# A margin on the PSUM banks in a hand-planned order of attention scores and a gated MLP

## The chip, the cores and the metric

The kernel runs on one core of a Trainium2 chip. The metric is device time in microseconds (us) for one execution, the median of several; lower is better. Three runs of the kernel before gave 2689.28, 2691.16 and 2694.49 us.

## The reference

One transformer-like block over 2048 rows of 576 columns, all in float32. The normalised rows go through an attention with 32 heads of 18 columns and, beside it, through a bilinear gated MLP with 4608 hidden columns; the two results are multiplied.

```python
def _A_ref(x, wqkv, wo):
    qkv = (x @ wqkv).reshape(B, S, 3, H, Dh) ...
    scores = jnp.einsum("bhqd,bhkd->bhqk", q, k) * (Dh ** -0.5)
    p = _softmax(scores, axis=-1)
    o = jnp.einsum("bhqk,bhkd->bhqd", p, v)
    return o.transpose(...).reshape(B, S, D) @ wo
def _B_ref(x, w_gate, w_up, w_down):
    g = jnp.einsum("bsd,df->bsf", x, w_gate)
    u = jnp.einsum("bsd,df->bsf", x, w_up)
    return jnp.einsum("bsf,fd->bsd", g * u, w_down)
xn = _layernorm(x)
return x + _A_ref(xn, A_wqkv, A_wo) * _silu(_B_ref(xn, B_w_gate, B_w_up, B_w_down))
```

## The kernel before

A first stage normalises the rows, projects q, k and v and writes them to DRAM. A last stage multiplies by `wo` and joins the two branches. Between them lies the main stage, from about 208 to 2610 us of the profiled execution, and everything that the change touches is in it.

Every float32 operand is carried as a high and a low part, so a product is a sum of three. In the main stage the 128 rows of the TensorE array are used as two halves of 64 rows, row group 0 and row group 64, which work at the same time on different matmuls. TensorE's instructions stand in one queue, and each matmul is preceded there by the load of its weights (LDWEIGHTS). The work of the stage is this:

- **First-pass scores** (`a_item`, L558): per head 64 matmuls of 54 rows by 512 columns into a PSUM bank `pa`, of which there are two, used in turn. VectorE reduces each bank to its row maxima (L560). A head's maxima are written back into the operand of the second pass (`max_rows`).
- **Second-pass scores** (`b_item`, L591): again 64 per head, into `pb`, also two banks in turn; ScalarE takes the exponential out of the bank (L593).
- **Up and gate products** (`gu_op`, L654): tiles of 27 matmuls of 512 columns into one of four banks `pg`; ScalarE (L659) or VectorE (L666) empties it. Row group 0 makes the up tiles, row group 64 the gate tiles.
- **Down products** (`down_op`, L682): tiles of 12 matmuls of 288 columns into a bank `pg`, which VectorE adds to the sums (L710; L708 for the first of a block).
- **Visits** (`visit`, `pv_group`, L602): the product of the exponentials with v, for four tiles of keys as a rule. These use the array in four column strips and not in two row groups, so both row groups stop for them. VectorE (L608) or ScalarE (L606) empties their `pg` bank.

A long matmul is one of 512 columns in a row group, a short one has 288 (`LONG, SHORT = 0.2335, 0.1335` at L783, in us).

**The order is planned when the program is built.** `order()` (L1010) keeps a clock for each row group (`clk`), the times at which VectorE, ScalarE and GpSimd will be free (`free`, `engine()`), and for each bank the time at which it may be used again (`banks`, `next_free()`). At each step it takes the row group whose clock is behind and emits one instruction for it: the next matmul of its stream (`stream()`: up or gate tiles and down tiles), or a score. The first-pass scores go to row group 0 and the second-pass scores to row group 64, with few exceptions. A score is emitted when its bank is free by the plan and its goal has come; the goals lie `pace` apart, so that the scores of all heads are spread over the stage (`a_goal`, `b_goal`). If neither can go, the clock is moved on. Nothing of the plan's times is in the program: what it leaves behind is the sequence on each engine, and on the chip each instruction waits for the semaphores of what it really needs. An instruction that waits holds what stands behind it in its queue.

Before the change a bank is usable 0.03 us after the plan's end of the operation that empties it, in four places (L883, L908, L960, L1056), and a score may be emitted up to 0.02 us ahead of that (L1042):

```python
banks["a"][slot] = engine("DVE", issue(r, LONG), 0.60) + 0.03      # L883
at, goal, score, can = next_free("a"), a_goal(na) + lean, a_next, na < TOTAL and na < nb + N + MOST   # L1032
blocked = op is not None and op[1] and next_free("g") > clk[r]     # L1041
```

The pace is worked out from a sum of the matmuls' lengths, `part`, and a term for the 512 (head, tile) pieces of the visits (L859 to L862).

Of the kernel before, what the change touches and what calls it, by code (L numbers as in the profile page):

```python
# [40 lines left out]
def kernel(  # L41
# [13 lines left out]
    H = 32  # L55
# [484 lines left out]
    with ExitStack() as mid:  # L540
# [283 lines left out]
        N = 64  # L824
        TOTAL = H * N
        LEAD, MOST = 24, 40
        PACE, SKEW, PULL, FIRST, ROWS = 1.01, 3.0, 3.0, 2.0, 6.0
        slots, gone = [0, 0], [0.0, 0.0]
        clk, free = [0.0, 0.0], {"DVE": 0.0, "ACT": 0.0, "POOL": 0.0}
# [10 lines left out]
        def engine(eng, start, taken):  # L840
            free[eng] = max(free[eng], start) + taken
            return free[eng] + TAIL[eng]

        def issue(r, length):

            at = issued[0] = max(clk[r], issued[0])
            clk[r] = at + length + (0.11 if fresh[r] else 0.0)
            fresh[r] = False
            return at + (0.456 if length == LONG else 0.356)
# [7 lines left out]
        there, queue = {}, [0.0]  # L857
        na = nb = 0
        part = len(units) * (2 * 27 * LONG + 4 * 12 * SHORT) + (TOTAL + N + LEAD) * LONG  # L859
        span = part + H * NT * (0.859 - 0.01)  # L860
        QUICK, LAST = 0.75, 0.75
        pace = (PACE * span - QUICK * N - LAST * (N + LEAD)) / (TOTAL - N)  # L862

# [8 lines left out]
        def a_next(r=0):  # L872
            nonlocal na
            h, i = divmod(na, N)
            if i == 0 and 2 <= h + 1 < H:
                stacks.append((0, h + 1))
            if i == 48 and (0, h + 1) in stacks:
                stacks.remove((0, h + 1))
                load_stack(0, h + 1)
            a_item(h, i, r)  # L880
            slot = turn["a"] % 2
            turn["a"] += 1
            banks["a"][slot] = engine("DVE", issue(r, LONG), 0.60) + 0.03  # L883
            na += 1
            if i == N - 1:
                max_fold(h)
                max_rows(h)
                rows_done[h] = engine("DVE", 0.0, 0.85) + ROWS
# [5 lines left out]
        def b_next(r=1):  # L894
            nonlocal nb
            h, i = divmod(nb, N)
            if i == 0 and h < H - 1:
                stacks.append((64, h + 1))
            if i == 48 and (64, h + 1) in stacks:
                stacks.remove((64, h + 1))  # L900
                load_stack(64, h + 1)
            if i == 16 and h % 2 == 0 and h // 2 + 1 < H // 2:
                load_v(h // 2 + 1)
            b_item(h, i, r)
            slot = turn["b"] % 2
            turn["b"] += 1
            end = engine("ACT", issue(r, LONG), 0.495)
            banks["b"][slot] = end + 0.03  # L908
            nb += 1
            if i % 4 == 3:  # L910
                due.append((h, i // 4, end + 0.03))
# [24 lines left out]
        def visit(now):  # L936

            now = max([now, *clk] + [j[0] for j in jobs])
            done = list(jobs)
            many = 0  # L940
            now += 0.095
            if due:
                now = max(now, next_free("g"))
            for j in done:
                jobs.remove(j)
                j[1](j[2])
                now += 0.6
                engine("DVE", now + 0.2, 0.8)
            for h, t, at in due:
                if at > now + 0.5 * many + 0.3 or h != due[0][0]:  # L950
                    break
                now += 0.859
                many += 1
            if many:
                k = banks["g"].index(next_free("g"))
                h = due[0][0]
                ts = [t for _, t, _ in due[:many]]
                pv_group(h, ts, k)
                end = engine("DVE", now + 0.25, 0.60) if ts[0] else engine("ACT", now + 0.25, 0.495)
                banks["g"][k] = end + 0.03  # L960
                if ts[-1] == NT - 1:
                    if h // 4 < H // 4 - 1:
                        finish(h)
                        engine("DVE", end, 1.45)
                    else:
                        jobs.append((end + 0.2, finish, h))
                del due[:many]
            clk[0] = clk[1] = issued[0] = now + 0.13
            fresh[:] = True, True
# [40 lines left out]
        def order():  # L1010
            nonlocal na, nb
            load_v(0)
            feeds = [stream(0), stream(1)]
            heads.extend(next(f) for f in feeds)
            wait = None
            while any(heads) or na < TOTAL or nb < TOTAL or due or jobs:
                now = max(clk)
                small(now)
                need = 4 if nb < TOTAL or any(heads) and not stuck[0] else 1
                if (len(due) >= need and due[need - 1][2] <= now  # L1020
                        or any(j[0] + (3.0 if due else 1.0) <= now for j in jobs)
                        or jobs and not any(heads) and na == TOTAL):
                    wait = now if wait is None else wait
                    if abs(clk[0] - clk[1]) < 0.04 or now > wait + 1.0 or not all(heads):
                        visit(now if any(heads) else max([now] + [j[0] for j in jobs] + [d[2] for d in due]))
                        wait = None
                        continue
                r = 0 if clk[0] <= clk[1] else 1
                lean = PULL * (gone[0] - gone[1] - SKEW) * (1 if r else -1)

                if r == 0 and (na < TOTAL or nb < TOTAL - N) or r == 1 and nb == 0 and na < N:
                    at, goal, score, can = next_free("a"), a_goal(na) + lean, a_next, na < TOTAL and na < nb + N + MOST  # L1032
                    can = can and not late(goal, r)
                else:
                    at, goal, score, can = next_free("b"), b_goal(nb) + lean, b_next, b_ready(r)
                op = heads[r]
                held = op is not None and not can_go(r, op[1], op[4])
                stuck[0] = held and heads[1 - r] is not None and not can_go(1 - r, heads[1 - r][1], heads[1 - r][4])
                if held:
                    op = None  # L1040
                blocked = op is not None and op[1] and next_free("g") > clk[r]  # L1041
                if can and (at <= clk[r] + 0.02 and (goal <= clk[r] or blocked) or op is None and (at <= clk[r] or not held)):  # L1042
                    clk[r] = max(clk[r], at)
                    score(r)
                elif op is not None:
                    length, first, work, end, (kind, n, k) = op
                    if first:
                        clk[r] = max(clk[r], next_free("g"))
                        slots[r] = banks["g"].index(next_free("g"))
                        banks["g"][slots[r]] = 1e9  # L1050
                    work()
                    lands = issue(r, length)
                    gone[r] += length
                    if end:
                        done = engine(end[0], lands, end[1])
                        banks["g"][slots[r]] = done + 0.03  # L1056
                        if kind == "d":
                            if k == 47:
                                parts.setdefault(n, []).append(clk[r])
                                if len(parts[n]) == 2:  # L1060
                                    downed[n] = moved(max(parts[n]) + 0.3, 1.18) if (n + 1) % NF2 else 0.0
                        elif r == 0:
                            upped[n] = done
                        else:
                            gated[n] = done
                            fin = engine("ACT", done + 0.05, 0.535)
                            fin = engine("POOL", fin + 0.05, 1.29)
                            loaded[n] = moved(done - 0.4, 1.18) if (n // 2 + 1) % NF2 else 0.0
                            lands = moved(fin, 0.524)
                            if n % 2:  # L1070
                                there["h", n // 2] = lands
                            if stacks:
                                load_stack(*stacks.pop(0))
                                moved(fin + 1.4, 0.88)
                    heads[r] = next(feeds[r], None)
                else:
                    clk[r] = max(clk[r] + 0.05, min(clk[1 - r] + 0.01, clk[r] + 0.3))
# [113 lines left out]
```

## Time and profile before

| | |
|---|---|
| runs of the kernel before | 2689.28, 2691.16, 2694.49 us |
| the profiled execution | 2687.2 us, of which 2685.4 us are its span |
| granted TensorE clock, mean | 0.997 |
| ScalarE L593, exponentials | 2048 of 597 ns, 1167.1 us busy |
| VectorE L560, maxima | 2048 of 685 ns, 1356.8 us busy |
| VectorE L710, down tiles | 544 of 445 ns, 233.4 us busy |

A row such as "L560 ... x2048 | 1356.8, 685" gives the line, the engine, what it writes and reads, how many there were, the busy time in us and the mean length of one in ns. PE is a matmul and PEld a weight load; the profiler models a matmul's end, so its start is the better number. In a timeline a row is a start, a length, an engine and a line, and rows of one kind that follow each other are merged ("x9"). In brackets stands how long the engine sat idle before, and what ended it. In the view of the waits a row gives who waited for whom, the sum in us, how often, and the longest; idle time under 0.15 us isn't listed there.

### The profile page before, as it was taken

The numbers are of one execution on the slowest core, as the hardware profiler recorded it, in microseconds if no ns is written. First come the engines' busy times: TensorE is split into PE (matmuls) and PEld (weight loads), VectorE is DVE, ScalarE is ACT, GpSimd is POOL, SyncE is SP. The second block draws the span as 40 slices with busy tenths as digits, with TensorE's granted clock in tenths as the row PEclk, the third lists the DMA queues.
The fourth block names the chain that finished last, engine by engine and source line by source line (L and its number), as shares of the span: only waits on it lengthen the run. The fifth ranks groups of instructions, "written<-read, shape, count | busy, mean of one in ns | idle before, by whom it ended". The sixth has DMA issues, their size and how long they took to land.

```text
span 2685.4 us, 59017 instructions
## 1 busy us (share of the span) xinstructions
PE 2649.1 (99%) x24456; PEld 2053.7 (76%) x24456; DVE 1917.8 (71%) x3384; ACT 1476.2 (55%) x2726; POOL 451.2 (17%) x414
## 2 busy tenths in 40 slices
PE   7999999999999999999999999999999999999998
PEld 5898777777777777777777777777777777777778
DVE  7217777777777787777777787777777787777536
ACT  3222666666665565565555555555555565555552
POOL 2113333333311111111001101000001111000005
PEclk9999999999999999999999999999999999999999
DMA  6799978888785656676676656566586565654555
GB/s 209 222 296 268 255 216 222 220 221 223 206 225 153 178 161 172 188 201 181 161 180 165 172 150 181 164 172 169 158 199 165 169 174 156 180 159 152 154 178 200
DMA packets 212820, 508.62 MB, mean 189 GB/s; under 512 B 71112, under 2 KB 130888, under 8 KB 179016
## 3 DMA queue, kind: packets, MB, share of 16 engines
q1 hardware_dynamic: 209512, 493.64, 65.9%
q0 software_dynamic: 3040, 11.21, 1.1%
q8 instruction: 192, 3.15, 0.5%
q14 instruction: 76, 0.62, 0.1%
HBM read 314.05 MB, written 109.97 MB: 158 GB/s over the span
## 4 chain that ended last, share of the span: by engine, by line
PE 93%; DVE 3%; DMA 2%; issue 1%; ACT 1%; POOL 1%; SPq 0%; POOLq 0%; ACTq 0%; DVEq 0%
PE pg L654 32%; PE pg L602 17%; PE pg L682 15%; PE pa L558 12%; PE pb L591 8%; PE pg L1148 2%; PE pg L373 2%; PE pa L319 2%; PE pb L319 2%; DMA xc<-sx 1%; DVE mx L560 1%; DVE xn L282 0%; DMA draw<-in_B_w_down_dram 0%; POOL wgu L192 0%; DVE st L271 0%
## 5 line engine op out<-in xcount | busy, mean ns | idle before, releaser
L593 ACT ACTIVATE pt<-pb 128x512 f32<-128x512 f32 x2048 | 1167.1, 597 | 686.6 <-PE pb L591 541.5
L560 DVE TENSOR_REDUCE mx<-pa 128x1 f32<-128x512 f32 x2048 | 1356.8, 685 | 247.4 <-PE pb L591 114.0
L654 PE MATMUL pg<-xc,wgu 64*128 64x512 f32 x7776 | 1387.8, 394 | 4.4 <-DMA xc<-sx 3.8
L654 PEld LDWEIGHTS pg<-xc,wgu 64*128 64x128 f32 x7776 | 993.3, 186 | 88.4 <-DMA xc<-sx 7.0
L558 PE MATMUL pa<-ks,qs 54*128 54x512 f32 x2048 | 830.4, 414 | 0.1
L591 PE MATMUL pb<-qs,ks 56*128 56x512 f32 x2048 | 820.0, 412 | 1.8 <-ACT pt L593 1.8
L682 PE MATMUL pg<-wd,hs 64*128 64x288 f32 x6816 | 775.3, 294 | 3.3 <-DVE acc L710 3.3
L682 PEld LDWEIGHTS pg<-wd,hs 64*128 64x128 f32 x6816 | 731.8, 185 | 28.6 <-issue 13.4
L558 PEld LDWEIGHTS pa<-ks,qs 54*128 54x128 f32 x2048 | 370.7, 184 | 168.0 <-issue 83.8
L670 POOL TENSOR_TENSOR hs<-us,hs 128x512 fp32r<-128x512 f32 x144 | 185.8, 1291 | 1804.9 <-ACT hs L669 1754.5
L602 PE MATMUL pg<-pt,vt 128*32 128x512 f32 x4096 | 466.4, 595 | 0.6 <-DVE acc L708 0.2
L591 PEld LDWEIGHTS pb<-qs,ks 56*128 56x128 f32 x2048 | 366.5, 184 | 27.4 <-ACT pt L593 10.8
L602 PEld LDWEIGHTS pg<-pt,vt 128*32 128x32 f32 x4096 | 119.8, 109 | 266.4 <-issue 260.0
L608 DVE TENSOR_TENSOR oc<-oc,pg 128x512 f32<-128x512 f32 x98 | 67.4, 688 | 310.0 <-PE pg L602 310.0
L710 DVE TENSOR_TENSOR acc<-acc,pg 128x288 f32<-128x288 f32 x544 | 233.4, 445 | 27.1 <-PE pg L682 25.0
L669 ACT ACTIVATE hs<-us 128x512 fp32r<-128x512 f32 x144 | 91.0, 632 | 159.0 <-DVE us L666 154.2
L192 POOL TENSOR_TENSOR wgu<-wraw,wgu 128x384 fp32r<-128x384 f32 x108 | 108.0, 1015 | 104.8 <-ACT wgu L191 76.5
L666 DVE TENSOR_TENSOR us<-pg,us 128x512 f32<-128x512 f32 x144 | 98.2, 682 | 23.2 <-PE pg L654 22.8
L659 ACT ACTIVATE us<-pg 128x512 f32<-128x512 f32 x144 | 86.1, 598 | 39.8 <-PE pg L654 27.7
L606 ACT ACTIVATE oc<-pg 128x512 f32<-128x512 f32 x32 | 19.1, 598 | 103.3 <-PE pg L602 103.3
L223 POOL TENSOR_TENSOR wd<-draw,wd 128x576 fp32r<-128x576 f32 x36 | 51.1, 1431 | 90.9 <-ACT wd L222 88.7
L323 DVE TENSOR_TENSOR hl<-pb,hl 128x512 fp32r<-128x512 f32 x18 | 12.4, 690 | 72.2 <-ACT hl L322 72.2
(104 smaller groups left out, 1071.3 us busy)
## 6 DMA issues: line engine op xcount, KB each, us to landing
wgu<-swg SPq DMA_DIRECT2D x102, 1152.0 KB
hs<-hs SPq DMA_DIRECT2D x288, 256.0 KB
wd<-swd SPq DMA_DIRECT2D x50, 1152.0 KB
swg<-wgu SPq DMA_DIRECT2D x36, 1152.0 KB
qs<-sqk SPq DMA_DIRECT2D x192, 144.0 KB
ks<-sqk SPq DMA_DIRECT2D x192, 144.0 KB
swd<-wd SPq DMA_DIRECT2D x18, 1152.0 KB
sqk<-hl SPq DMA_DIRECT2D x32, 512.0 KB
```

The source lines that it names most:

```text
L192: nc.gpsimd.tensor_tensor(w[:, 9 + b:12 + b, :], raw[:, b:b + 3, :], w[:, b:b + 3, :].bitcast(FT), op=OP.subtract)
L319: nc.tensor.matmul(p, wq[b, a], xcs[c][:, e, :], start=n == 0, stop=n == len(PAIRS) - 1)
L558: nc.tensor.matmul(p, q[rows, t * 128:(t + 1) * 128], k[rows, c * 512:(c + 1) * 512], start=True, stop=True)
L560: nc.vector.tensor_reduce(mx[h][:, t, c:c + 1], p, axis=AX.X, op=OP.max)
L591: nc.tensor.matmul(p, k[rows, t * 128:(t + 1) * 128], q[rows, c * 512:(c + 1) * 512], start=True, stop=True)
L593: nc.scalar.activation(pt[t, c // 2][:, c % 2, :], p, AF.Exp, scale=scale)
L602: nc.tensor.matmul(p[32 * c:32 * c + 32, :], vt[h // 2][:, t, 6 * (h % 2):6 * (h % 2) + 32], pt[t, c // 2][:, c % 2, :], start=t == ts[0], ...
L654: nc.tensor.matmul(ps, gw[n][half[r], a, :], xg[i][half[r], e, :], start=k == 0, stop=k == len(TERMS) - 1)
L666: nc.vector.tensor_tensor(h32, ps, h32, op=OP.mult)
L670: nc.gpsimd.tensor_tensor(hj[:, 1, :], h32, hj[:, 0, :].bitcast(FT), op=OP.subtract)
L682: nc.tensor.matmul(ps[:, 0:HALF], hs[u][half[r], k, j, a, s * 128:(s + 1) * 128], dw[u][half[r], k, j, e, :], start=n == 0, stop=n == len( ...
L710: nc.vector.tensor_tensor(a, a, ps[:, 0:HALF], op=OP.add)
```

## The change

A constant `EARLY = 0.17` takes the place of 0.03 at the four places where a bank's next use is noted. The tolerance for a score falls from 0.02 to 0.01 us. `visit` takes the margin off again where it sets its own time. In the pace, the length of a visit's piece is taken as 0.859 - 0.04 and not 0.859 - 0.01 us, so that `span` is 512 x 0.03 = 15.4 us shorter and two scores' goals lie about 0.008 us closer together (1.01 x 15.4 / 1984). No instruction is added or removed in number: the same matmuls, evictions and transfers are emitted, in another order.

```diff
+        EARLY = 0.17
...
-        span = part + H * NT * (0.859 - 0.01)
+        span = part + H * NT * (0.859 - 0.04)
...
-            banks["a"][slot] = engine("DVE", issue(r, LONG), 0.60) + 0.03
+            banks["a"][slot] = engine("DVE", issue(r, LONG), 0.60) + EARLY
...
-            banks["b"][slot] = end + 0.03
+            banks["b"][slot] = end + EARLY
...
             if due:
-                now = max(now, next_free("g"))
+                now = max(now, next_free("g") - EARLY + 0.03)
...
-                banks["g"][k] = end + 0.03
+                banks["g"][k] = end + EARLY
...
-                if can and (at <= clk[r] + 0.02 and (goal <= clk[r] or blocked) or op is None and (at <= clk[r] or not held)):
+                if can and (at <= clk[r] + 0.01 and (goal <= clk[r] or blocked) or op is None and (at <= clk[r] or not held)):
...
-                        banks["g"][slots[r]] = done + 0.03
+                        banks["g"][slots[r]] = done + EARLY
```

## The prediction

> **What bounds the kernel now.** I read the page first, then the groups by line, the waits, the chain and timelines of some microseconds.
>
> ```profile
> span 2685.4 us, 59017 instructions
> ...
> PE 2649.1 (99%) x24456; PEld 2053.7 (76%) x24456; DVE 1917.8 (71%) x3384; ACT 1476.2 (55%) x2726; POOL 451.2 (17%) x414
> ...
> PEclk9999999999999999999999999999999999999999
> ...
> PE 93%; DVE 3%; DMA 2%; issue 1%; ACT 1%; POOL 1%; SPq 0%; POOLq 0%; ACTq 0%; DVEq 0%
> ...
> L560 DVE TENSOR_REDUCE mx<-pa 128x1 f32<-128x512 f32 x2048 | 1356.8, 685 | 247.4 <-PE pb L591 114.0 <-PE pa L558 106.5 <-PE pg L654 17.2
> L654 PE MATMUL pg<-xc,wgu 64*128 64x512 f32 x7776 | 1387.8, 394 | 4.4 <-DMA xc<-sx 3.8
> L558 PE MATMUL pa<-ks,qs 54*128 54x512 f32 x2048 | 830.4, 414 | 0.1
> L591 PE MATMUL pb<-qs,ks 56*128 56x512 f32 x2048 | 820.0, 412 | 1.8 <-ACT pt L593 1.8
> L682 PE MATMUL pg<-wd,hs 64*128 64x288 f32 x6816 | 775.3, 294 | 3.3 <-DVE acc L710 3.3
> ```
>
> TensorE's order is the bound: 93% of the chain, at full granted clock; VectorE at 71% comes next. But a PE busy to 99% isn't PE at its best. What the main stage would need with no wait at all is worked out from starts, since the ends are modelled:
>
> ```profile
> 618.99 1.31 PE L654 MATMUL pg<-xc,wgu 64*128 64x512 f32 x9
> 633.84 1.06 PE L682 MATMUL pg<-wd,hs 64*128 64x288 f32 x12
> 626.80 3.57 PE pg L602 x32
> ...
> L654 PE MATMUL pg<-xc,wgu x7776: 383/392/792, 207.8 to 2583.5; 64*128 64x512 f32 x200
> ...
> 2603.73 6.24 PE L682 MATMUL pg<-wdl,hs 64*128 64x288 f32 x90
> ```
>
> Nine long matmuls, two row groups at work: (1.31 - 0.39) / 8 x 2 = 0.23 us from one to the next of a row group. Short ones: (1.06 - 0.29) / 11 x 2 = 0.14. The kernel's own constants, 0.2335 and 0.1335, agree, and I use them. A full visit (16 matmuls, each shown as two) takes 3.57. Laying the planned sequence of TensorE out with these lengths, each instruction after the one before it in its row group and not ahead of the one before it in the queue, and with no wait of any kind, gives 2313 us from the first L654 to the last L682. The trace has these at 207.8 and 2603.73 + 6.24 = 2610, so 2402 us. The 89 us between are the most that a better order of the same instructions could win. The waits view shows where weight loads are held:
>
> ```profile
> PEld pa L558 <- DVE mx L560: 55.2, 250, 0.5
> PEld pb L591 <- ACT pt L593: 10.8, 43, 1.3
> PEld pg L654 <- DMA xc<-sx: 7.0, 8, 1.7
> PEld pg L682 <- DVE acc L710: 5.1, 8, 1.8
> PEld pg L602 <- DVE acc L710: 4.0, 16, 0.5
> ```
>
> The wait for a score's bank stands at the **load of its weights**, not at its matmul. 250 of the 2048 first-pass scores and 43 of the second-pass ones are held there. What one costs, beside one that isn't held:
>
> ```profile
> 605.90 0.18 PEld L558 LDWEIGHTS pa<-ks,qs 54*128 54x128 f32 x1
> 606.14 0.39 PE L558 MATMUL pa<-ks,qs 54*128 54x512 f32 x1
> ...
> 614.70 0.39 PE L591 MATMUL pb<-qs,ks 56*128 56x512 f32 x1
> 614.94 0.18 PEld L558 LDWEIGHTS pa<-ks,qs 54*128 54x128 f32 x1 [0.15 <-DVE mx L560]
> 614.94 0.50 PE L558 MATMUL pa<-ks,qs 54*128 54x512 f32 x1
> 614.94 0.29 PEld L654 LDWEIGHTS pg<-xc,wgu 64*128 64x128 f32 x2
> ```
>
> At 605.90 the load goes ahead by 0.24 us, a whole long slot, under the matmul before it in the row group. At 614.94 VectorE's release comes so late that load and matmul are shown at one time and the matmul reads 0.50 instead of 0.39: its true start is 0.11 later. The other group's load (L654) stood behind it in the queue and also began at 614.94. So a bank that becomes free just when the matmul is due is 0.11 us too late, and both row groups lose it.
>
> **The change part by part.**
>
> *The two score banks.* How soon can a bank be used again? From a score to its eviction:
>
> ```profile
> 605.00 0.39 PE L591 MATMUL pb<-qs,ks 56*128 56x512 f32 x1
> 605.43 0.60 ACT L593 ACTIVATE pt<-pb 128x512 f32<-128x512 f32 x1 [0.16 <-PE pb L591]
> ...
> 314.38 0.68 DVE L666 TENSOR_TENSOR us<-pg,us 128x512 f32<-128x512 f32 x1
> 315.10 0.63 ACT L669 ACTIVATE hs<-us 128x512 fp32r<-128x512 f32 x1 [1.07 <-DVE us L666]
> ```
>
> 0.43 us from start to start, then 0.685 of reduce, then some 0.04 until the next engine moves (315.10 - 315.06): 1.16 us, all but five long slots (5 x 0.2335 = 1.168). A score five slots behind the last on its bank has its load released exactly when its matmul is due, and pays the 0.11. In the order before, 269 first-pass scores stand under 1.2 us behind the last one on their bank, nearly the 250 holds of the view; in the changed order none stands under 1.26 us, and 551 stand at six slots (1.40), against 267 before. For the second pass the count under 1.2 us goes from 326 to 87; ScalarE's 0.60 instead of 0.685 makes five slots nearly enough there, hence only 43 listed holds. The margin of 0.17 is thus the 0.11 that a load needs ahead of its matmul and a little more.
>
> Price: 250 + 43 holds by 0.11 us = 32 us. Bounds: the view's idle sum, 55.2 + 10.8 = 66 us, is the most these holds can cost; nothing is the least, if each is paid again somewhere else. I take 32, since it is the matmul's delay and not the load's idle time that counts. Holds under 0.15 us, which the view leaves out, would add to it; those left in the new order take away; I set these against each other.
>
> *What fills the gap.* A score put off by a slot lets the next L654 or L682 of that row group through; nothing stands idle for it. The same layout of the changed order comes to 2312 us against 2313, so the price in idle slots is nil. That isn't free of doubt: places where two instructions of one row group follow each other in the queue rise from 1257 to 1475. If that cover were gone, each would cost up to one slot of the other group, 218 x 0.13 to 0.23 = 28 to 51 us.
>
> *The pg banks.* These hold little (5.1 + 4.0 us of idle above, with the visits' share), so the margin wins at most 9 us there; I take nothing, since holds of up to 1.8 us are too long to be cured by 0.14.
>
> *Visits.* 131 runs of L602 in the new order against 130. Around one the loads pause:
>
> ```profile
> 608.56 0.16 PEld L602 LDWEIGHTS pg<-pt,vt 128*32 128x32 f32 x8 [0.36 <-issue]
> ```
>
> One more costs about 0.36 and a held first load, 0.5 us. This also checks the 32: of the 89 us missing, 130 pauses of 0.36 make 47 and the DMA holds 7, which leaves 35 for the score banks.
>
> *The pace.* Goals 0.008 us closer bring the last first-pass score forward: after it stand 324 L654 and 425 L682 in the new order, 231 and 384 in the old, (93 x 0.2335 + 41 x 0.1335) / 2 = 13.6 us. TensorE has work of other kinds to the end (85 against 82 second-pass scores follow), and VectorE's load rises by under 1%: 1357 us of reduces in 2299 instead of 2313 us. Cost nil in the layout.
>
> *The transfers* come 1% closer together; the DMA holds above (7.0 us) may grow by a few us, in the range.
>
> Sum, against the profiled execution's 2687.2 us (its span and 1.8 around it): -32 + 0.5 = 2655.5. The median of the runs lies 4.0 above the profiled one: **2659 us**.
>
> The Trainium skill speaks against this change in one place. TensorE: Matmul & The Clock Gate, in its section on row and column tiling, says that the 64-deep queue pulls a weight load ahead when it is for a row group that isn't in conflict. By that rule the load of the other row group would pass a held one, a hold would cost one group of two, and the margin would be worth nearer 16 than 32 us. The trace doesn't agree for a load held by a semaphore: at 614.94 the L654 load began with the held one, after 0.15 us in which no load ran.
>
> **The rivals.**
>
> *Half of it comes back* (0.23). The plan holds a reduce for 0.60 us and the trace has 0.685; where VectorE also has L710 and L666 in hand, a bank comes later than plan and margin say, and the holds move to six slots. For it: the longest hold is 0.5 us, beyond any margin of 0.17. Against: the mean listed hold is 55.2 / 250 = 0.22 us of the load's idle, and the load has 0.13 us to give (0.24 - 0.11). Half the gain left: 2687.2 - 16 + 4 = 2675.
>
> *Nothing changes* (0.05). If the 0.11 is lost under a slot that was idle in any case, the order is worth the same: 2691. For it: the two layouts are equal. Against: the 35 us that visits and DMA leave over.
>
> *The down tiles run short of banks* (0.08). Two of four pg banks are being filled all the time; in a stretch of down tiles each row group wants a new one every 12 x 0.1335 = 1.60 us. One comes back after 0.43 + 0.445, and where a reduce stands ahead on VectorE 0.685 more: 1.56 us, plus 0.05. With 0.14 on top that is 1.75, over 1.60, so the plan makes a row group stop. 576 tile starts by 0.14 us, two groups side by side: 40 us, more than the 32 won: 2687.2 - 32 + 40 + 4 = 2699. It decides from the point at which more than four in five starts meet that edge. For it: the 1475 same-group neighbours. Against: only 8 holds at L682, and the equal layouts.
>
> **How the numbers follow.** The likeliest (0.64) has its own range of 2644 to 2670: 66 instead of 32 can't come whole, since the load's idle overlaps running matmuls, so I allow 47 on one side and 21 on the other. The measurement tells 0.2%, some 5 us, from no change. Faster holds the likeliest and the half, 0.87; same 0.05; slower 0.08. For 8 in 10 the range goes up through the half case to 2684 and down to 2643.
>
> **What would show it.** The row PEld pa L558 <- DVE mx L560 falls from 250 times to under 80; L558 and L591 matmuls' means fall from 414 and 412 ns toward the 394 of L654; the visits come closer together from early on, evenly over the main stage, and not in one place. It is wrong if L682 or L602 take over as held loads (over 20 us), if the holds at L558 stay above 150, or if the L682 of the last stretch end at 2600 us or later.

## The result and the profile after

| | before | after |
|---|---|---|
| median | 2690.49 us (2689.28 to 2694.49, 4 runs) | 2649.73 us (2648.21 to 2650.84, 4 runs) |
| ratio | | 0.9846, 95% interval 0.9829 to 0.9863 |
| profiled execution, span | 2687.2, 2685.4 us | 2649.72, 2648.0 us |

The change wins 41 us by the medians and 37.5 between the two profiled executions; 32 had been forecast. The matmuls are the same in number, but the new order has 131 visits instead of 130, and so VectorE has one operation more (3385). First the page of the changed kernel: span, busy time of the engines, shares of the chain, and the groups that answer to those shown of before.

```profile
span 2648.0 us, 58984 instructions
...
PE 2608.8 (99%) x24456; PEld 2104.5 (79%) x24456; DVE 1913.4 (72%) x3385; ACT 1468.6 (55%) x2726; POOL 452.7 (17%) x414
...
PE 95%; DVE 3%; DMA 1%; issue 0%; ACT 0%; POOL 0%; SPq 0%; ACTq 0%; DVEq 0%
...
L560 DVE TENSOR_REDUCE mx<-pa 128x1 f32<-128x512 f32 x2048 | 1357.2, 685 | 198.6 <-PE pb L591 94.5
L654 PE MATMUL pg<-xc,wgu 64*128 64x512 f32 x7776 | 1409.7, 391 | 0.8 <-ACT vo L379 0.5
...
L682 PE MATMUL pg<-wd,hs 64*128 64x288 f32 x6816 | 811.9, 293 | 9.5 <-DMA wd<-swd 8.6
L558 PE MATMUL pa<-ks,qs 54*128 54x512 f32 x2048 | 802.0, 401 | 1.7 <-DVE mx L560 1.7
L591 PE MATMUL pb<-qs,ks 56*128 56x512 f32 x2048 | 803.3, 404 | 0.0
```

No operation became quicker: L560 takes 685 ns as before, L654 391 against 394. What shrank is the mean length of a score's matmul, 414 to 401 and 412 to 404 ns, the sign of a matmul that is shown with its load and starts late. TensorE is 99% busy in both kernels, so its busy share says nothing of the 37 us. The weight loads show them; this is the view of the waits after the change (us in total, times, longest):

```profile
PEld pg L682 <- DMA wd<-swd: 9.0, 1, 9.0
...
PEld pa L558 <- DVE mx L560: 6.3, 23, 1.8
...
PEld pg L682 <- DVE acc L710: 1.9, 5, 0.8
...
PEld pb L591 <- ACT pt L593: 1.6, 8, 0.3
```

The loads held for a first-pass bank fell from 250 (55.2 us) to 23 (6.3), those for a second-pass bank from 43 to 8. A timeline of the changed kernel has a normal score and one of the 23:

```profile
614.85 0.18 PEld L558 LDWEIGHTS pa<-ks,qs 54*128 54x128 f32 x1
...
615.07 0.39 PE L558 MATMUL pa<-ks,qs 54*128 54x512 f32 x1
...
615.34 0.22 DVE L566 TENSOR_REDUCE m<-mx 128x16 f32<-128x64 f32 x1
...
615.60 1.18 DVE L573 TENSOR_SCALAR mm<-m 128x16 fp32r<-128x16 f32 x1
...
617.87 0.18 PEld L558 LDWEIGHTS pa<-ks,qs 54*128 54x128 f32 x1 [0.75 <-DVE mx L560]
```

The first load goes 0.22 us ahead, as an unheld one did before. The second follows a head's end, where L573 took 1.18 us (in the profile of before 24 of its 32 took 0.17 to 0.18 us, and four took 1.18 to 1.19), while the plan has 0.85 for all four operations there: no margin of 0.17 covers that.

The time came from the whole stage. The first visit starts 4 us earlier than before, the 21st 8, the 61st 29, the 101st 38 and the last 35 us earlier, read from the first L602 of each. One new wait took something back. At the turn to the third block of rows the down weights arrive late:

```profile
1377.08 0.34 SPq L216 DMA_DIRECT2D wd<-swd  x1
...
1391.40 0.29 PEld L682 LDWEIGHTS pg<-wd,hs 64*128 64x128 f32 x1 [8.99 <-DMA wd<-swd]
```

In the kernel before, six loads for x were held at the same turn (5.2 of the 7.0 us of its row xc<-sx); the other two stood at the next turn.

### The profile page after: what moved, and what is told of

The parts are those of the page before. It is cut to its first block, busy times and chain, and to the rows that moved or that the text cites. A ratio compares the mean times of both kernels' runs of the same rounds, so it can differ in the third digit from the quotient of the medians.

```text
span 2648.0 us, 58984 instructions
## 1 busy us (share of the span) xinstructions
PE 2608.8 (99%) x24456; PEld 2104.5 (79%) x24456; DVE 1913.4 (72%) x3385; ACT 1468.6 (55%) x2726; POOL 452.7 (17%) x414
## 4 chain that ended last, share of the span: by engine, by line
PE 95%; DVE 3%; DMA 1%; issue 0%; ACT 0%; POOL 0%; SPq 0%; ACTq 0%; DVEq 0%
PE pg L654 34%; PE pg L602 17%; PE pg L682 15%; PE pa L558 12%; PE pb L591 8%; PE pg L1149 2%; PE pg L373 2%; PE pa L319 2%; PE pb L319 2%; DMA wd<-swd 1%; DVE mx L560 0%; DVE xn L282 0%; DMA xc<-sx 0%; DVE st L271 0%; DMA sqk<-hl 0%
## 5 line engine op out<-in xcount | busy, mean ns | idle before, releaser
L560 DVE TENSOR_REDUCE mx<-pa 128x1 f32<-128x512 f32 x2048 | 1357.2, 685 | 198.6 <-PE pb L591 94.5
L654 PE MATMUL pg<-xc,wgu 64*128 64x512 f32 x7776 | 1409.7, 391 | 0.8 <-ACT vo L379 0.5
L654 PEld LDWEIGHTS pg<-xc,wgu 64*128 64x128 f32 x7776 | 1057.6, 186 | 56.2 <-DMA xc<-sx 1.2
L682 PE MATMUL pg<-wd,hs 64*128 64x288 f32 x6816 | 811.9, 293 | 9.5 <-DMA wd<-swd 8.6
L558 PE MATMUL pa<-ks,qs 54*128 54x512 f32 x2048 | 802.0, 401 | 1.7 <-DVE mx L560 1.7
L591 PE MATMUL pb<-qs,ks 56*128 56x512 f32 x2048 | 803.3, 404 | 0.0
L682 PEld LDWEIGHTS pg<-wd,hs 64*128 64x128 f32 x6816 | 767.3, 185 | 27.1 <-DMA wd<-swd 9.0
L602 PE MATMUL pg<-pt,vt 128*32 128x512 f32 x4096 | 468.3, 597 | 1.2 <-DVE acc L708 0.8
L602 PEld LDWEIGHTS pg<-pt,vt 128*32 128x32 f32 x4096 | 120.0, 110 | 269.0 <-issue 264.8
L710 DVE TENSOR_TENSOR acc<-acc,pg 128x288 f32<-128x288 f32 x544 | 236.5, 445 | 29.9 <-PE pg L682 28.3
L659 ACT ACTIVATE us<-pg 128x512 f32<-128x512 f32 x144 | 86.1, 598 | 30.2 <-PE pg L654 24.7
```

Source lines behind the costliest of these rows:

```text
L558: nc.tensor.matmul(p, q[rows, t * 128:(t + 1) * 128], k[rows, c * 512:(c + 1) * 512], start=True, stop=True)
L560: nc.vector.tensor_reduce(mx[h][:, t, c:c + 1], p, axis=AX.X, op=OP.max)
L591: nc.tensor.matmul(p, k[rows, t * 128:(t + 1) * 128], q[rows, c * 512:(c + 1) * 512], start=True, stop=True)
L602: nc.tensor.matmul(p[32 * c:32 * c + 32, :], vt[h // 2][:, t, 6 * (h % 2):6 * (h % 2) + 32], pt[t, c // 2][:, c % 2, :], start=t == ts[0], ...
L654: nc.tensor.matmul(ps, gw[n][half[r], a, :], xg[i][half[r], e, :], start=k == 0, stop=k == len(TERMS) - 1)
L682: nc.tensor.matmul(ps[:, 0:HALF], hs[u][half[r], k, j, a, s * 128:(s + 1) * 128], dw[u][half[r], k, j, e, :], start=n == 0, stop=n == len( ...
```

## The experiments

All twelve start from the kernel before. Its four places carry one of three constants (first-pass banks, second-pass banks, pg banks), so that each can be set alone; `visit` subtracts the pg constant and adds 0.03 as in the change. Each diff shows what differs from 0.03, the tolerance of 0.02 and the pace of 0.859 - 0.01.

A waits view lists idle of 0.15 us and more. For these runs I also counted in each trace all score loads that started **too late**: with less than 0.095 us left of the slot of the matmul before them in their row group, so that their own matmul had to start late. The mark of 0.095 lies a little below the 0.11 that the prediction read. The counts depend on it, the picture doesn't: 908 became 345 by this mark, 1064 became 408 by a mark of 0.11, 612 became 156 by one of 0.06. Not every late load waits for a bank: 237 of the 908 stood over 1.6 us behind the last score on theirs, in the layout without waits.

The experiments were measured in three sets, and each ratio in the table is to runs of the kernel before in the same set (medians 2688.59, 2688.54 and 2689.39 us; 2690.49 for the change itself).

| run | margin first / second / pg | too late, first + second pass | median, us | ratio, 95% interval |
|---|---|---|---|---|
| before | 0.03 / 0.03 / 0.03 | 427 + 481 | 2688.5 to 2690.5 | |
| t1_tol_only | as before, tolerance 0.01 | 301 + 450 | 2679.64 | 0.9967 (0.9957 to 0.9977) |
| t3_pace_alone | as before, new pace | 413 + 474 | 2689.50 | 1.0006 (0.9997 to 1.0016) |
| e2_pg_only | 0.03 / 0.03 / 0.17, new tolerance and pace | 331 + 452 | 2687.19 | 0.9996 (0.9987 to 1.0005) |
| a1_first_only | 0.17 / 0.03 / 0.03 | 148 + 432 | 2662.90 | 0.9907 (0.9892 to 0.9922) |
| a2_second_only | 0.03 / 0.17 / 0.03 | 447 + 281 | 2683.07 | 0.9980 (0.9970 to 0.9989) |
| a3_scores_both | 0.17 / 0.17 / 0.03 | 133 + 242 | 2663.79 | 0.9908 (0.9891 to 0.9924) |
| a4_first_pg | 0.17 / 0.03 / 0.17 | 146 + 403 | 2667.36 | 0.9917 (0.9902 to 0.9932) |
| a5_second_pg | 0.03 / 0.17 / 0.17 | 463 + 299 | 2684.38 | 0.9981 (0.9972 to 0.9991) |
| t2_margin_only | 0.17 / 0.17 / 0.17 | 145 + 237 | 2650.16 | 0.9857 (0.9842 to 0.9871) |
| after | 0.17 / 0.17 / 0.17, new tolerance and pace | 133 + 212 | 2649.73 | 0.9846 (0.9829 to 0.9863) |
| d10_margin | 0.10 three times | 254 + 309 | 2664.51 | 0.9912 (0.9897 to 0.9926) |
| d24_margin | 0.24 three times | 72 + 50 | 2646.03 | 0.9839 (0.9824 to 0.9854) |
| d30_margin | 0.30 three times | 53 + 35 | 2657.93 | 0.9884 (0.9869 to 0.9898) |

### Which of the three edits: tolerance, margin, pace

```diff
# t1_tol_only
-                if can and (at <= clk[r] + 0.02 and (goal <= clk[r] or blocked) or op is None and (at <= clk[r] or not held)):
+                if can and (at <= clk[r] + 0.01 and (goal <= clk[r] or blocked) or op is None and (at <= clk[r] or not held)):
```

> Only the tolerance for a score falls from 0.02 to 0.01 us; margin (0.03) and pace stay as before. In its order the first-pass scores under 1.2 us behind the last one on their bank fall from 269 to 34, while the second-pass ones stay at 330 (326 before). If a hold costs 0.11 us for each such pair, this alone wins 235 x 0.11 = 26 us: about 2665. If it is the margin of 0.17 that counts, since a bank that is free just as planned still comes 0.11 too late for the load, at most a third of the gain appears: 2677 to 2690.

```diff
# t2_margin_only
+        EARLY_A, EARLY_B, EARLY_G = 0.17, 0.17, 0.17
```

> Only the margin: 0.17 at all four places, with the old tolerance of 0.02 and the old pace. First-pass pairs under 1.2 us: 0; second-pass: 95. By the theory that late weight loads are the whole of it, all of the gain is here: 2648 to 2656, as in the changed kernel. If the pace carries a part, 5 to 15 us of the gain are missing: 2656 to 2666.

```diff
# t3_pace_alone
-        span = part + H * NT * (0.859 - 0.01)
+        span = part + H * NT * (0.859 - 0.04)
```

> Only the pace: the visits' piece at 0.859 - 0.04 instead of 0.859 - 0.01; margin and tolerance as before. First-pass pairs under 1.2 us: 292 (269 before), second-pass 345 (326). Theory: no gain, 23 + 19 more holds at up to 0.11 us make it 0 to 5 us slower, 2690 to 2695. Rival, that closer goals fill the end of the stage better: 5 to 15 us faster.

The margin alone gives the whole gain, 2650.16 us; the pace alone gives nothing that can be told from 1. The tolerance alone is the surprise. The order it makes has 34 first-pass scores under 1.2 us behind the last on their bank, where the one before had 269, and yet it wins 9 us (6 to 12 by its interval) and not 26. The waits of the run with the tolerance alone:

```profile
PEld pa L558 <- DVE mx L560: 18.2, 80, 0.7
...
PEld pb L591 <- ACT pt L593: 9.8, 31, 2.7
```

Listed holds fell from 293 to 111. But of 908 loads that came too late 751 were left, 652 of them not in the view's list, against 677 before: the edit took away listed holds and left the short ones. A score that the plan puts a slot later, but again at the very time its bank becomes free, can still have its load come too late. Of the first-pass scores six slots behind the last on their bank (1.3 to 1.45 us in the layout), 92 of 566 were late in this run, and 16 of 589 in the run with the margin alone.

### Which of the three kinds of bank

```diff
# e2_pg_only (with the tolerance and the pace of the change)
+        EARLY_A, EARLY_B, EARLY_G = 0.03, 0.03, 0.17
```

> The margin of 0.17 on the four pg banks alone; the score banks stay at 0.03; tolerance 0.01 and the new pace. First-pass pairs under 1.2 us: 35, second-pass 342. It is to be read against the run with the tolerance alone: the theory gives the pg banks nothing (their holds made 9.1 us of idle in all), so within 5 us of that run. Rival, that the down tiles' banks carry part of the gain: 8 us or more faster than that run; or slower by as much, if the margin makes the plan stop a row group at the down tiles.

```diff
# a1_first_only
+        EARLY_A, EARLY_B, EARLY_G = 0.17, 0.03, 0.03
```

> Margin 0.17 on the two first-pass banks alone; second-pass and pg banks at 0.03, old tolerance and pace. In the trace of the kernel before, 427 first-pass and 481 second-pass loads start so late that their matmul starts late (counted from the starts, listed as waits or not); in the changed kernel 133 and 212. If each of the 563 fewer has one price, 41 / 563 = 0.07 us, this part wins about 290 x 0.07 = 20 us: 2668. Rival, that the two passes run in step and a held load of either holds the other's: 10 us or less alone, 2678 or more, and the whole only with both.

```diff
# a2_second_only
+        EARLY_A, EARLY_B, EARLY_G = 0.03, 0.17, 0.03
```

> Margin 0.17 on the two second-pass banks alone; the rest as before. One price for each late load: about 270 x 0.07 = 19 us, 2669. Rival, both in step: 10 us or less, 2678 or more. By the waits view alone (43 listed holds of 293) it would be 5 us: 2684.

```diff
# a3_scores_both
+        EARLY_A, EARLY_B, EARLY_G = 0.17, 0.17, 0.03
```

> Margin 0.17 on the first-pass and second-pass banks, 0.03 on the pg banks; old tolerance and pace. Theory: all of the gain, 2648 to 2654. Rival, the pg banks carry a part: 2656 or more.

```diff
# a4_first_pg
+        EARLY_A, EARLY_B, EARLY_G = 0.17, 0.03, 0.17
```

> Margin 0.17 on the first-pass and the pg banks, 0.03 on the second-pass banks; old tolerance and pace. The first pass alone gave 2662.9, both passes 2663.8, all three 2650.2. If the pg banks carry a share of their own, some 13 us: about 2650, and the second pass adds nothing. If only the three together do it, 2660 to 2664.

```diff
# a5_second_pg
+        EARLY_A, EARLY_B, EARLY_G = 0.03, 0.17, 0.17
```

> Margin 0.17 on the second-pass and the pg banks, 0.03 on the first-pass banks; old tolerance and pace. The second pass alone gave 2683.1. If the pg banks carry some 13 us of their own: about 2670. If their share appears only once the first-pass scores no longer hold the queue: 2678 to 2686.

The run with the margin on the pg banks, and the new tolerance and pace, came out 7.6 us slower than the tolerance alone, and not within 5 us of it. Its trace puts 5.8 us of that behind the main stage: what follows the last L682 took 81.2 us against 75.4 in the run with the tolerance alone, with this hold in it:

```profile
PEld pb L1126 <- DMA oin<-so: 5.2, 1, 5.2
```

The run with the pace alone has it too (3.8 us, and 80.1 us behind the main stage), so the pg margin isn't needed for it. The changed kernel, which also has the new pace, has no such hold and took 75.2 us there.

The first-pass banks alone win 25.6 us and the second-pass banks alone 5.5: together 31, and roughly in the proportion of the holds that the view of before lists, 250 to 43. One price for every late load had been expected to give 2668 and 2669 us; the second pass alone stands at 2683.07, where the listed holds had put it (2684). These are the weight loads held for a score's bank in the run with the first-pass margin alone, the second-pass row first:

```profile
PEld pb L591 <- ACT pt L593: 7.0, 37, 0.4
...
PEld pa L558 <- DVE mx L560: 2.4, 8, 1.1
```

and in the one with the second-pass margin alone:

```profile
PEld pa L558 <- DVE mx L560: 65.2, 268, 0.9
...
PEld pb L591 <- ACT pt L593: 4.2, 10, 1.2
```

Each margin cleared its own banks and left the others held. 242 listed first-pass holds went for 25.6 us, 0.106 us each, and 33 second-pass ones for 5.5, 0.17 each.

The trace of the kernel before gives the price of a hold more directly. From starts alone, the matmuls before and behind a first-pass score with a listed hold lie 0.09 us further apart on average than their slots (median 0.11), and those of the other row group beside it 0.14 us (median 0.07). Where a score's load is late but not listed, it is 0.07 to 0.09 us in its own row group and 0.05 in the other; beside scores that aren't late, it is 0.01 and at most 0.03. In none of 286 listed holds did one of the next five loads in the queue start ahead of the held one. So a listed hold does cost both row groups, as the prediction took it, and a shorter one costs mostly its own.

The parts don't add up further, though. Both score margins together (2663.79) are no better than the first alone, and not the 2648 to 2654 that had been expected. The pg margin put on top of one pass makes that run no faster: 0.9917 against 0.9907 of the kernel before, and 0.9981 against 0.9980. Yet all three together win 13.6 us more than the two, and there the intervals lie apart (0.9842 to 0.9871 and 0.9891 to 0.9924). I added up, in each trace, the single waits of over 0.3 us of the main stage's weight loads, outside visits, that something released: 26.4 us with both score margins, 16.5 with all three, 18.5 with the first pass alone, 18.4 before. With both score margins 9.8 us of it are holds for x at two turns between blocks of rows, and 3.1 are long first-pass holds elsewhere:

```profile
PEld pg L654 <- DMA xc<-sx: 9.8, 14, 1.4
...
PEld pa L558 <- DVE mx L560: 7.9, 29, 1.6
```

With all three margins the first of these rows is smaller, and the longest hold of the second is short:

```profile
PEld pg L654 <- DMA xc<-sx: 5.5, 7, 1.6
PEld pa L558 <- DVE mx L560: 5.3, 29, 0.2
```

So up to 10 of the 13.6 us are such long waits (the idle time of a load is the most that its matmul can lose), and the layout of the order without waits differs by another 1.2 (2315.8 against 2314.6). The long waits also fit the other surprise: the run with both margins has 190 fewer late second-pass loads than the first pass alone, and 8 us more of long waits. Whether the pg margin spares these waits, or whether one order meets the transfers better than another by chance, these runs don't settle; the two pairs in which it made nothing better speak for chance, but no order was drawn anew with its margins kept.

### How large a margin

```diff
# d10_margin, d24_margin, d30_margin: 0.10, 0.24 and 0.30 in all three
+        EARLY_A, EARLY_B, EARLY_G = 0.10, 0.10, 0.10
```

> Margin 0.10 instead of 0.17 at all four places; old tolerance and pace. Theory: a load needs its bank 0.11 us ahead of the matmul and some 0.04 to 0.05 for the semaphore, so 0.03 is short by 0.12 and 0.10 by 0.05: some 60% of the gain, 2662 to 2670. Rival, that all that counts is a plan with five slots or fewer between two uses of a bank: 28 and 221 such pairs stand in this order (269 and 326 before, 0 and 95 with 0.17), so nearly all for the first pass, half for the second, 2662 to 2675; the two part at the count of late loads, under 0.05 each by the theory, 0.10 by the rival.

> Margin 0.24 at all four places, old tolerance and pace: one long slot, so that a load can start a whole slot ahead, as an unheld one does. Second-pass pairs under 1.2 us: 14 (95 with 0.17). Theory: 0.17 already covers what a load needs (0.11 and 0.04 to 0.05 for the semaphore), so within 5 us of 2650. Rival, that every bit of lead counts: 2635 to 2643.

> Margin 0.30 at all four places, old tolerance and pace. The order changes its rhythm: first-pass pairs at six slots fall from 565 to 34, seven slots take their place, and same-group neighbours rise to 1710. Theory: nothing more to win, and nothing lost while the layout stays (2314.9 us): 2647 to 2657. Rival, that spreading the scores is what wins: 2640 or less; or that pushed-off scores break the pairing of the row groups: over 2660.

From 0.03 over 0.10, 0.17 and 0.24 the median goes from 2688.5 over 2664.5 and 2650.2 to 2646.0, and the loads that come too late from 908 over 563 and 382 to 122. With 0.10 the time is in the range of both expectations, and 345 fewer late loads for 24.0 us are 0.07 us each, between the 0.05 and the 0.10 that should have parted them. The step from 0.17 to 0.24 stays within the 5 us that were allowed for it. With 0.24 the main stage takes 48 us more than its layout without waits, where it took 89 more before and 52 in the changed kernel. The 48 are little more than the 47 us that the prediction puts down for the pauses at visits. At 0.30 only 88 loads are late and the time is back at 2657.9, 1 us above the range expected. The waits of that run name the down tiles:

```profile
PEld pg L682 <- DVE acc L710: 8.5, 11, 2.2
...
PEld pg L682 <- DMA wd<-swd: 7.9, 2, 7.7
...
PEld pg L682 <- DVE us L666: 2.9, 4, 1.4
...
PEld pg L682 <- DVE acc L708: 2.0, 3, 1.2
```

For the run with 0.24 the same view has:

```profile
PEld pg L682 <- DVE acc L710: 4.2, 6, 1.1
...
PEld pg L682 <- DVE us L666: 0.7, 1, 0.7
...
PEld pg L682 <- DMA wd<-swd: 0.2, 1, 0.2
```

Held for a bank that VectorE empties: 8.5 + 2.9 + 2.0 = 13.4 us against 4.9; held for down weights: 7.9 against 0.2. Idle time of the loads is an upper bound of what the matmuls lose, and the medians lie 12 us apart. By these rows the banks of the down tiles, a rival in the prediction, do become a cost, but only with a margin of 0.30. Two things stand beside it and weren't taken apart. The late weights may be chance: the run with 0.17 and otherwise the same has none, but the changed kernel has 9.0 us of them. And neighbours of one row group rose to 1710, from 1376 with 0.24.

The kernel with 0.24 is the lowest of all, 2646.03 us (2644.03 to 2647.05), against 2650.16 with 0.17 and otherwise the same (2649.98 to 2650.77). They were measured in different sets, and the intervals of their ratios overlap (0.9824 to 0.9854 and 0.9842 to 0.9871), so a gain of 0.1 to 0.2% is likely but not shown.

## Why the prediction was right, and where it was not

- **The mechanism held.** The wait of a score stands at its weight load, and an order that frees the bank earlier in the plan takes the wait away: the margin alone has the whole gain, and 293 listed holds became 33 in that run and 31 in the changed kernel. Both row groups lose time at a listed hold, as the starts above show; the 16 us that the prediction set against its 32 needed a load of the other group to pass a held one, and none did.
- **The size came out partly by luck.** The term for the two score banks, 250 + 43 holds by 0.11 us = 32, measured 25.6 + 5.5 = 31 us with each margin by itself, but 24.7 with both set together. The term for the pg banks, nil, measured 13.6 us on top of these two. One term was 7 us too large, the other 14 too small, and the sum came within 6 to 9 us of what the whole change brought. Up to 10 of the 13.6 are single long waits, which the prediction didn't count at all. The sum itself has a small slip: 2687.2 - 32 + 0.5 is 2655.7 and not 2655.5; nothing hangs on it.
- **The holds too short to be listed were mis-sized.** The prediction set them against those that would remain. There were 908 late loads, 677 of them not in the list, and the tolerance alone shows how far the list misleads: 182 listed holds fewer, which at 0.11 would be 20 us, won 9. But a count of all late loads gives no single price either: 0.06 us for each of 157 fewer with the tolerance alone, 0.07 with the whole change, 0.08 with the first pass alone (328 fewer), 0.03 with the second (180 fewer).
- **The picture of the five slots was half of it.** It fits the listed holds: 214 of the 250 first-pass ones stand under 1.2 us behind the last score on their bank. But of the 908 late loads, 437 do. With the tolerance alone 235 of the 269 first-pass pairs were gone and a quarter of the gain came. Scores six slots behind were late too where the plan left them no margin.
- **Tolerance.** The prediction gave it no term. Alone it wins 9 us; beside the margin nothing is seen of it: 2650.16 with the old one and the old pace, 2649.73 with the new ones. That comparison also holds the 9.0 us of late down weights, which only the changed kernel has.
- **Nil for the pg banks** was wrong as a size, by 13.6 us beside both score margins, and right beside either of them alone. Why stays open, as said above. The rival that the down tiles run short did not arise at 0.17: L682's holds for L710 went from 5.1 to 1.9 us.
- **Nil for pace and gap-filling** held: the pace alone measured 1.0006. In its trace the main stage is 2.8 us shorter and what follows it 4.8 us longer. The layouts without waits were equal, and the margin alone, with 1272 neighbours of one row group, is no faster than the change with 1475, so these cost nothing that could be seen.
- **Transfers** held up the changed kernel by 9 us at one place, where another transfer held 5.2 before; all holds for transfers at L654 and L682 went from 7.0 to 10.2, so "a few us more" was about right.
- **The rival that half comes back** didn't arise: 23 first-pass holds were left, though the longest, 1.8 us, is beyond any margin, as it said.

## What to carry to other kernels

When the order of work is fixed by a plan, the time at which a bank is *needed* is that of the first instruction that waits for it, here the weight load, some 0.1 us and up to a slot ahead of its matmul; plan against that and not against the matmul. Size the margin by trying it in both directions: it cost nothing that could be seen here up to 0.24, while other work filled the slot, and at 0.30 the time rose again. Set the parts together as well as one by one: here they didn't add up. And count stalls from the starts of the instructions: a list of waits with a threshold shows some of the holds, and an edit that takes those away can leave most of the late loads where they were.

## What was not expected of the hardware

- A weight load held by a semaphore cost about 0.1 us in its row group though the bank became free about when the matmul was due (0.09 on average for the listed first-pass holds of before, and 0.14 in the other row group). TensorE's busy share stayed at 99% with 908 such late loads as with 345. The mean length of the matmul, 414 against 401 ns, showed it better than the busy share.
- Taking 0.01 us off the plan's tolerance left 235 fewer first-pass scores five slots behind the last on their bank, and won 9 us of 2690. The plan's edge and the slots lay that close: 1.168 us for five slots against a bank that the plan frees 0.456 + 0.60 + 0.095 + 0.03 = 1.181 us after the score begins (its constants at L849, L883 and L830).
- VectorE's L573 took 0.17 to 0.18 us in 24 of its 32 uses before, and 1.18 to 1.19 in four; the cause wasn't looked for.
